# Two transformer layers on one core: query blocks outermost, heads in row and column tiles, three-bank exponentials, and the FFN and next QKV of a finished block run beside the next block's attention

## The chip, the cores and the metric

The kernel runs on one core of a Trainium2 chip. The time is the device time in microseconds (us) of one execution. Engines are named as in the profile: PE is the matmul engine (TensorE), PEld its weight loads, DVE is VectorE, ACT is ScalarE, POOL is GpSimd, SP is SyncE. Each timed run lies beside runs of the kernel before on the same chip.

## The reference, cut to what matters

Two equal layers, each of attention (16 heads of 28) and an FFN with a squared ReLU, over 2048 tokens of width 448; both layers use the same weights.

```python
def attention(x, wqkv, wo):                   # x: 2048 x 448
    q, k, v = split((x @ wqkv), 3, heads=16)  # 16 x 2048 x 28 each
    p = softmax(q @ k.T * 28 ** -0.5)         # 16 x 2048 x 2048
    return merge_heads(p @ v) @ wo
def ffn(x, w1, b1, w2, b2):                   # inner width 1792
    return relu(x @ w1 + b1) ** 2 @ w2 + b2
x = x + attention(layernorm(x), ...);  x = x + ffn(layernorm(x), ...)   # twice
```

The exponentials alone are 2 x 16 x 2048 x 2048 elements: over 128 partitions, 1,048,576 columns for ACT.

## The kernel before: the parts that matter

Each layer is four stages, one after the other: layernorm and QKV, attention, output projection, FFN. Attention goes head by head. A head's 28 query rows are copied into a zeroed buffer of 128 rows, so that a score matmul can use all 128 rows of a K buffer that holds four heads.

```python
order = [(h, kb, u) for h in range(H) for kb in range(NKB) for u in range(NU)]
def issue_scores(h, kb, u):                            # 1024 queries: two banks
    for j in range(2):                                 # L280
        nc.tensor.matmul(sc[:, j*512:(j+1)*512], lhsT=QK_sb[:, mk, kb*P:(kb+1)*P],
                         rhs=qz[:, qc*512:(qc+1)*512], start=True, stop=True)
for i, (h, kb, u) in enumerate(order):
    sc = pending
    pending = issue_scores(*order[i + 1])
    nc.scalar.activation(out=pt, in_=sc, func=AF.Exp, scale=scale)     # L312
    for j in range(2):                                 # L315, column tile by query block
        nc.tensor.matmul(oT[32*qc:32*qc+32, 0:512], lhsT=V_sb[:, kb, h, 0:DHP],
                         rhs=pt[:, j*512:(j+1)*512], tile_position=(0, 32*qc), ...)
# ... cut: head normalisation, a few late QKV tiles ...
attention_layer(); ffn_layer(); attention_layer(); ffn_layer()
```

The softmax here doesn't subtract the row's maximum and nothing guards it: scores larger than these inputs give would overflow.

## Time and profile before

The median is 1514.76 us in 3 runs (1514.45 to 1515.83).

| | before |
|---|---|
| span of the profiled run | 1513.1 us |
| PE, ACT, DVE busy | 89%, 75%, 28% |
| mean granted PE clock | 0.981 |
| in the two attention stages | 1153 us: PE 90%, ACT 87% |
| in all other stages | 360 us, without one exponential |

The busy shares of the page are averages over stages with different limits. The windows by stage, quoted in the prediction, take them apart.

### The profile page before, as it was taken

What the parts mean: (1) busy time and instruction counts of PE and PEld (TensorE: products, weight loads), DVE (VectorE), ACT (ScalarE), POOL (GpSimd) and SP (SyncE); (2) the same over time, 40 slices, a digit from 0 to 9 for tenths busy, and PEclk for the clock granted to TensorE, in tenths of its full rate; (3) what the DMA queues carried; (4) which work ended last, traced back from release to release, by engine and by line L of the source; (5) the groups of instructions that cost most, each with busy time, mean ns of one, the idle gap of its engine ahead of it and who ended that gap; (6) DMA issues with size and microseconds to landing.
All of it is one profiled execution on the core that took longest, in us unless ns stands there. A gap on an engine that the chain in (4) does not pass through costs nothing.

```text
span 1513.1 us, 15919 instructions
## 1 busy us (share of the span) xinstructions
PE 1351.2 (89%) x6214; PEld 438.0 (29%) x6320; DVE 428.9 (28%) x783; ACT 1137.6 (75%) x1273; POOL 29.3 (2%) x41
## 2 busy tenths in 40 slices
PE   6999988888888888699999998888888888887998
PEld 2222222222222222233332222222222222223333
DVE  7333211122111111564452332221111111116432
ACT  4678899988999988354347888899999999882432
POOL 6000000000000000000000000000000000000000
PEclk8999999999999999889999999999999999997999
DMA  6000000000000000110000000000000000002000
GB/s 124 1 0 1 1 1 0 1 0 1 0 1 1 0 1 0 44 43 0 1 1 0 1 1 1 0 1 1 0 1 0 1 0 1 0 1 86 13 16 22
DMA packets 20212, 13.92 MB, mean 9 GB/s; under 512 B 10089, under 2 KB 19242, under 8 KB 20138
## 3 DMA queue, kind: packets, MB, share of 16 engines
q1 hardware_dynamic: 18922, 9.76, 2.6%
q0 software_dynamic: 1216, 3.16, 0.8%
q8 instruction: 49, 0.80, 0.2%
q14 instruction: 25, 0.20, 0.0%
HBM read 11.07 MB, written 1.84 MB: 9 GB/s over the span
## 4 chain that ended last, share of the span: by engine, by line
PE 67%; ACT 24%; issue 5%; DVE 3%; ACTq 0%; DMA 0%; POOL 0%; SPq 0%; POOLq 0%
PE sc L280 25%; ACT pt L312 24%; PE oT L315 16%; PE ph L393 7%; PE py L411 5%; PE pq L208 4%; PE den_b L337 2%; PE pq L224 2%; PE tp L181 2%; PE py L355 2%; DVE st L140 1%; PE oT L332 1%; PE oT L301 1%; PE py L418 1%; DVE recip L341 0%
## 5 line engine op out<-in xcount | busy, mean ns | idle before, releaser
L312 ACT ACTIVATE pt<-sc 128x1024 bf16<-128x1024 f32 x1024 | 1000.1, 1022 | 142.3 <-PE sc L280 126.4
L280 PE MATMUL sc<-qz,QK_sb 128*128 128x512 bf16 x1963 | 603.5, 385 | 0.3 <-issue 0.2
L315 PE MATMUL oT<-pt,V_sb 128*32 128x512 bf16 x2048 | 403.9, 385 | 110.8 <-ACT pt L312 108.7
L315 PEld LDWEIGHTS <-V_sb 128*32 128x32 bf16 x2048 | 152.9, 92 | 518.5 <-issue 518.5
L266 DVE MEMSET qz<- 128x1024 uint32 x32 | 29.2, 912 | 559.5 <-PE sc L280 558.6
L280 PEld LDWEIGHTS <-QK_sb 128*128 128x128 bf16 x2048 | 117.7, 97 | 235.6 <-issue 235.0
L401 ACT ACTIVATE rtmp<-ph,b1col 128x512 bf16<-128x512 f32 x112 | 76.7, 686 | 93.6 <-PE ph L393 93.6
L393 PE MATMUL ph<-xnT,w 128*128 128x512 bf16 (+1 forms) x432 | 124.4, 394 | 1.8 <-issue 0.7
L341 DVE RECIPROCAL recip<-den_b 128x512 f32<-128x512 f32 x32 | 107.4, 3357 | 27.7 <-PE den_b L337 27.5
L411 PE MATMUL py<-w,hact 128*128 128x448 bf16 x448 | 91.0, 353 | 0.0
L208 PE MATMUL pq<-xnT,wqk 128*128 128x512 bf16 (+1 forms) x251 | 83.3, 394 | 3.0 <-ACT xnT L189 1.4
L216 DVE CAST QK_sb<-pq 128x512 bf16<-128x512 f32 x60 | 41.3, 688 | 126.4 <-PE pq L208 126.3
L335 DVE COPY oT_sb<-oT 128x512 f32<-128x512 f32 x32 | 22.1, 692 | 164.5 <-PE oT L332 164.5
L404 DVE TENSOR_TENSOR hact<-rtmp 128x512 bf16<-128x512 bf16 x112 | 47.2, 424 | 65.2 <-ACT rtmp L401 65.2
L181 PE MATMUL tp<-ident,xn 128*128 128x128 bf16 (+1 forms) x256 | 36.8, 261 | 30.3 <-ACT xn L163 28.5
L393 PEld LDWEIGHTS <-w 128*128 128x128 bf16 x448 | 34.7, 97 | 86.6 <-issue 72.7
L411 PEld LDWEIGHTS <-hact 128*128 128x128 bf16 x448 | 40.9, 98 | 41.5 <-issue 7.1
L144 ACT ACT_TABLE_LOAD x3 | 3.8, 1283 | 57.6 <-DVE mv L142 57.6
L208 PEld LDWEIGHTS <-wqk 128*128 128x128 bf16 (+1 forms) x256 | 24.3, 98 | 50.7 <-issue 31.1
L140 DVE BATCH_NORM_STATS2 st<-x_sb 128x6 f32<-128x448 bf16 x64 | 38.3, 607 | 1.3 <-DMA x_sb<-in_A_x_dram 0.8
L163 ACT ACTIVATE xn<-x_sb,nbias,rstd 128x448 bf16<-128x448 bf16 x32 | 24.3, 760 | 19.0 <-PE tp L181 12.7
L224 PE MATMUL pq<-wv,xnT 128*128 128x448 bf16 (+1 forms) x128 | 35.5, 370 | 1.6 <-DVE V_sb L231 1.4
(48 smaller groups left out, 400.9 us busy)
## 6 DMA issues: line engine op xcount, KB each, us to landing
w<-in_B_w_dram SPq DMA_DIRECT2D x2, 1568.0 KB, 12.2
x_sb<-in_A_x_dram SPq DMA_DIRECT2D x4, 448.0 KB
w<-in_B_w_dram POOLq DMA_DIRECT2D x4, 448.0 KB, 7.1
wo_pad<-in_A_wo_dram SPq DMA_DIRECT2D x4, 392.0 KB
w<-in_B_w_dram SPq DMA_DIRECT2D x2, 448.0 KB, 4.5
out_dram<-x_sb SPq DMA_DIRECT2D x8, 112.0 KB, 1.7
out_dram<-x_sb POOLq DMA_DIRECT2D x8, 112.0 KB, 1.9
w<-in_B_w_dram SPq DMA_DIRECT2D x2, 224.0 KB, 6.7
```

The lines of the kernel that those rows point to most:

```text
L140: nc.vector.bn_stats(out=st[:, :], in_=x_sb[:, tb, :])
L181: nc.tensor.transpose(out=tps[dc][:r, j * P:(j + 1) * P], in_=xn[:, dc * P:dc * P + r], identity=ident[:, :],)
L208: nc.tensor.matmul(pq[:, :], lhsT=wqk[0:r, dc, m, :], rhs=xnT[0:r, dc, tcix * 512:(tcix + 1) * 512], start=(dc == 0), stop=(dc == NDC - 1),)
L224: nc.tensor.matmul(pv[:, 0:D], lhsT=xnT[0:r, dc, tb * P:(tb + 1) * P], rhs=wv[0:r, dc, :], start=(dc == 0), stop=(dc == NDC - 1),)
L280: nc.tensor.matmul(sc[:, j * 512:(j + 1) * 512], lhsT=QK_sb[:, mk, kb * P:(kb + 1) * P], rhs=qz[:, qc * 512:(qc + 1) * 512], start=True, s ...
L312: nc.scalar.activation(out=pt[:, :], in_=sc[:, :], func=AF.Exp, scale=scale)
L315: nc.tensor.matmul(oT[32 * qc:32 * qc + 32, 0:512], lhsT=V_sb[:, kb, h, 0:DHP], rhs=pt[:, j * 512:(j + 1) * 512], start=False, stop=False, ...
L341: nc.vector.reciprocal(out=recip[:qrows, :], in_=den_b[:qrows, :])
L393: nc.tensor.matmul(ph[:, :], lhsT=w1[0:r, dc, fc * P:(fc + 1) * P], rhs=xnT[0:r, dc, tcix * 512:(tcix + 1) * 512], start=(dc == 0), stop=( ...
L401: nc.scalar.activation(out=rtmp[:, :], in_=ph[:, :], func=AF.Relu, bias=b1col[:, fc:fc + 1], scale=1.0)
L404: nc.vector.tensor_tensor(out=hact[:, :], in0=rtmp[:, :], in1=rtmp[:, :], op=ALU.mult)
L411: nc.tensor.matmul(py2[:, :], lhsT=hacts[fc][:, j * P:(j + 1) * P], rhs=w2[:, fc, :], start=(fc == 0), stop=False,)
```

## The change

Its intent is to keep ACT at the exponentials from the first to the last. The loop over blocks of 512 queries goes outermost. Four heads lie in four groups of 32 partitions, so that score matmuls of three heads can run in three row tiles and PV matmuls in three column tiles. An exponential covers three PSUM banks (1536 columns). When a query block's attention is done, its projection, FFN and the next layer's QKV are merged into the instruction stream of the next block's attention, by a planner inside the kernel that runs when the program is built and fixes each engine's order. The kernel shares out eight PSUM banks: six for scores, one for the PV sums (`ps_o`), and one (`ps_m`) for all other matmul tiles, which I call filler tiles.

```diff
-order = [(h, kb, u) for h in range(H) for kb in range(NKB) for u in range(NU)]
+    for l in range(2):
+        cut = 4 if l == 0 else NTB - 4
+        for qb in range(NQB):
+            if qb == 0:        # first block: K of the blocks that are ready, then the rest
+                for lo, hi in ((0, cut), (cut, NTB)):
+                    for g in range(G):
+                        passes.append((l, qb, g, range(lo, hi), lo == 0, hi == NTB))
+            else: ...
+    groups = [units[i:i + 3] for i in range(0, len(units), 3)]
...
-            rhs=qz[:, qc * 512:(qc + 1) * 512],
+                r = slice(DHP * hh, DHP * hh + DHP)                       # L416
+                nc.tensor.matmul(sc[:, k * 512:(k + 1) * 512],
+                                 lhsT=K_sb[l][r, g, kb * P:(kb + 1) * P],
+                                 rhs=Q_sb[l][r, g, qb * QB:(qb + 1) * QB],
+                                 start=True, stop=True, tile_position=(DHP * hh, 0))
...
-    nc.scalar.activation(out=pt[:, :], in_=sc[:, :], func=AF.Exp, scale=scale)
+    nc.scalar.activation(out=pt[:, 0:n], in_=gbuf[gi]["sc"][:, 0:n], func=AF.Exp, scale=scale)  # L431, n = 1536
...
+                nc.tensor.matmul(box["t"][DHP * hh:DHP * hh + DHP, :],    # L460
+                                 lhsT=V_sb[l][:, kb, 4 * g + hh, :],
+                                 rhs=gbuf[gi]["pt"][:, k * 512:(k + 1) * 512], ...,
+                                 tile_position=(0, DHP * hh))
...
+    def chain(l, qb):          # spawned when a query block is normalised
+        # projection, layernorm, FFN; in layer 0 also layernorm and QKV of layer 1
+        ...
+    # a filler tile: matmuls into the one bank of ps_m (L335), then its evacuation
...
+        nc.gpsimd.memset(V_sb[0][:], 1.0)                                 # L199
+        nc.gpsimd.memset(V_sb[1][:], 1.0)                                 # L214
```

Smaller parts of it: weights are loaded once and not per layer, b1 is a row of w1, 1/sqrt is done on DVE instead of ACT, and the transposes of a half block share one bank.

## The prediction

> **What bounds the kernel now.** I read the windows by stage first, cut where the exponentials (L312) begin and end: head, attention, output projection, layernorm and FFN, layernorm and QKV, attention, projection, FFN. Columns: stretch, its length, then busy time of PE, PEld, DVE, ACT, POOL.
>
> ```profile
> 0.00:38.00 38.00, 23.24 (x97) 8.98 (x98) 27.81 (x94) 15.81 (x35) 22.74 (x29) 0.87 0.67 123
> 38.00:617.00 579.00, 520.90 (x2227) 158.47 (x2271) 122.71 (x131) 501.41 (x513) 0.00 (x0) 1.00 0.00 1
> 617.00:638.00 21.00, 15.55 (x266) 7.61 (x263) 13.77 (x20) 0.00 (x0) 1.12 (x2) 0.84 0.05 9
> 638.00:766.00 128.00, 120.82 (x535) 45.80 (x543) 66.35 (x196) 56.60 (x100) 0.00 (x0) 0.95 0.08 25
> 766.00:788.00 22.00, 19.48 (x106) 8.26 (x106) 16.55 (x53) 12.54 (x26) 0.00 (x0) 1.00 0.00 0
> 788.00:1362.00 574.00, 516.89 (x2207) 156.63 (x2249) 117.43 (x122) 499.02 (x512) 0.00 (x0) 1.00 0.00 1
> ```
>
> Two attention stages take 1153 us of 1513; PE is busy 90% there and ACT 87%, so neither is free. The other 360 us (38+21+128+22+22+129) run with no exponential at all. Then the costliest groups, which size the units of work, and the chain of waits:
>
> ```profile
> PE 67%; ACT 24%; issue 5%; DVE 3%; ACTq 0%; DMA 0%; POOL 0%; SPq 0%; POOLq 0%
> ...
> L312 ACT ACTIVATE pt<-sc 128x1024 bf16<-128x1024 f32 x1024 | 1000.1, 1022 | 142.3 <-PE sc L280 126.4
> L280 PE MATMUL sc<-qz,QK_sb 128*128 128x512 bf16 x1963 | 603.5, 385 | 0.3 <-issue 0.2
> L315 PE MATMUL oT<-pt,V_sb 128*32 128x512 bf16 x2048 | 403.9, 385 | 110.8 <-ACT pt L312 108.7
> ```
>
> ACT waits 142 us, nearly all for scores; PE waits 111 us for exponentials. They hand work to each other and both lose. The timeline of one steady stretch (start, duration) shows how:
>
> ```profile
> 300.32 0.39 PE L315 MATMUL oT<-pt,V_sb 128*32 128x512 bf16 x2 [0.26 <-ACT pt L312]
> ...
> 300.65 0.61 PE L280 MATMUL sc<-qz,QK_sb 128*128 128x512 bf16 x2
> ...
> 301.24 0.39 PE L315 MATMUL oT<-pt,V_sb 128*32 128x512 bf16 x2
> 301.35 1.94 ACT L312 ACTIVATE pt<-sc 128x1024 bf16<-128x1024 f32 x2 [0.17 <-PE sc L280]
> ```
>
> Two exponentials run without a gap in 1.94 us, so the second starts 0.92 us after the first; then 0.17 us is lost. Start to start on PE, two PV matmuls cost 0.33 us (their two column tiles overlap), two score matmuls 0.59 us (0.54 in the chain), one after the other. PE needs about 0.89 us per unit of 1024 columns and ACT 0.92; with each waiting for the other, 577/512 = 1.13 us results.
>
> Two pieces of the chain of waits carry the cost of tiled and untiled matmuls outside attention: 256 matmuls of the output projection, four row tiles at a time, and 14 of the FFN's second product.
>
> ```profile
> 621.91 14.13 PE py L355 x231
> ...
> 673.00 2.75 PE py L411 x14
> ```
>
> **What the Trainium skill says.** (1) "ScalarE: Activation LUTs", What ACT_TABLE_LOAD costs: 186 ns plus 0.833 ns per element, neighbours overlapping by about 93 ns. The trace agrees closely: 1022 ns at 1024 columns (formula 1039), overlap 100 ns. (2) "TensorE: Matmul & The Clock Gate", Measured speedup vs the span model: four row tiles with a contraction of 32 gave 3.07 times. This trace has such matmuls, the output projection L355 (32 rows, 448 columns): 14.13 us / 64 = 0.22 us per four (the trace lacks a few records, the program has 256), where L411, of the same width, takes 2.75 / 14 = 0.196 each. That is 3.6 times. (3) "TensorEngine Tiling (Array Packing)", Key Properties: a change of tiling mode drains TensorE. The trace fits: L393 needs 1.07 us per four matmuls, one of them on 64 rows; four at 0.22 (L411's rate scaled to 512 columns) would be 0.89, so about 0.1 us per change. (4) The first page, part 3, The mechanism: matmuls start and end in program order. So a merged matmul that waits for its PSUM buffer holds up the scores behind it. The kernel before has little of that to check.
>
> **The change, part by part.** Instruction counts come from the two programs' orders.
>
> Exponentials: 1024 of 1024 columns become 683 of 1536. By the trace's slope, 1.02 + 512 x 0.833 ns = 1.45 us each, 1.35 us start to start. 683 x 1.35 = **922 us**, against 1024 x 0.92 = 942 before if it never waited. The width alone saves only 20 us.
>
> Attention on PE: the scores keep 2048 matmuls, but with 32 rows, three heads side by side: 0.22 + 0.11 for the mode change = 0.33 us instead of 3 x 0.27 = 0.81. PV: three column tiles for about 0.36. So 0.69 us per group, 471 us in all, where 1024 x 0.89 = 911 us stood. The zero-padded queries (32 memsets, 64 copies on DVE) go. ACT becomes the bound with half of PE free.
>
> What fills that half: transposes 256 x 0.08 = 20, QKV 256 x 0.216 + 128 x 0.196 = 80, projection 25, FFN 448 x 0.216 + 480 x 0.196 = 191, denominators 32 x 0.86 = 28: 344 us. About 60 of these lie in the tail and in stalls below; some 285, in about 370 of the 683 groups, lie beside exponentials. PE there: 471 + 285 + 370 x 0.2 (two changes of mode) = 830 of 922 us. It fits on average, but a group with filler has 0.69 + 0.76 + 0.2 = 1.65 us against 1.35. If all that excess counted it would be 370 x 0.3 = 111 us; two score buffers and filler-free neighbours should take half. I add **50 us**.
>
> Stages that stay outside: the order shows where score groups stop for fillers. All fillers share one PSUM bank, so each is serial: 0.87 matmuls + 0.65 evacuation + 0.25 handoff, about 1.8 us.
> - First exponential: first x at 6 us, four statistics 3, rsqrt by twelve small DVE operations 2, normalise, transpose and evacuate twice 6, K and Q of four heads 5: **22 us**.
> - Layer 1 needs K of all blocks at once. Before score group 5, six tiles are serial (11 us against 7 us of exponentials); after group 25 seven tiles (12.6 less 2.7 us queued on ACT); after group 31 eleven (20 less 2.7). Stalls 4 + 10 + 17 = **31 us**.
> - Between layers, after group 351: the rest of an FFN, a layernorm, one K tile, 13 less 2.7; after group 404: two FFN output tiles (2 x 3.75), layernorm 8, K 1.8, less 2.7. **10 + 14 = 24 us**.
> - Tail after the last exponential: PV, copy, denominator 2.3; reciprocal 3.4; multiply 0.7; projection 4 x 1.6; layernorm 8; FFN 14 x 1.75 and 4 x 3.75; output 4.6 (as before, from last addition to end): **65 us**.
>
> Sum: 22 + 922 + 50 + 31 + 24 + 65 = 1114; I state **1110 us**. As a balance: the 360 us without exponentials shrink to 142, attention from 1153 to 972.
>
> **Rivals.** (a) PE becomes the bound. For: 830 of 922 us is 90%, and PE can't reorder past a waiting matmul. Against: row tiles ran at 3.6 times here. If three row tiles ran serially (0.75 us per group), PE would need 1.1 us before fillers, 1120 us in all beside 922: total about 1290. (b) The single PSUM bank for fillers becomes the bound, with DVE behind it: 304 tiles x 1.8-3.8 us and a 3.36 us reciprocal holding it 32 times make 304 x 2.2 + 32 x 4 = 800 us, close enough to ACT to stop PE in places; I'd give it 30 to 60 us more, 1150-1170. (c) Planned order fits better than I think, fillers fully hidden: 1060. (d) DVE as the bound: adding its groups at the durations before (relu 0.69, square 0.42, evacuations 0.69, reciprocals 107 in all) gives about 520 us, half the span; no. (e) Transfers: 9 GB/s mean, and weights are loaded once rather than per layer; they only matter in the head.
>
> **Range and chances.** (c) sets the lower end, (b) the upper: 1055 to 1170. Even serial row tiles leave 15%, so slower needs a fault I don't see.
>
> **What would show it right or wrong.** Right: ACT busy about 990 us (683 x 1.45) and near 10 tenths in the middle of the span; L431 idle for PE about 100-130 us, most of it in the first 110 us and at two gaps midway; score triples in 0.33 us; ACT leading the chain; about 65 us after the last exponential. Wrong: score triples near 0.7 us or PE above 95% busy through the middle (rival a); PE idle behind evacuations spread over the whole span (b); the head's and midway's stalls twice or half my 55 us, as that is counted from an order with durations of another kernel; exponentials not overlapping by 0.1 us (683 x 0.1 = 68 us more).

## The result, and the profile after

The kernel after takes 1145.82 us (median of 4 runs, 1143.03 to 1147.52); the kernel before took 1514.61 us beside it. The ratio is 0.7565, with a 95% interval from 0.7551 to 0.758. Ratios here are the mean time of one kernel's runs over that of the other's of the same rounds, so they are not quite the ratio of the medians. The forecast was 1110 us, within 1055 to 1170: the direction and most of the size are right, and 36 us are missing.

From the page of the kernel after: PE, ACT and the granted clock in 40 slices, then the three groups of attention.

```profile
PE   2876878889898989899789967999889988899646
ACT  1763899999999999999579738899989999899511
PEclk9998876899898998899889978699969986799569
...
L431 ACT ACTIVATE pt<-sc 128x1536 bf16<-128x1536 f32 (+1 forms) x683 | 926.3, 1538 | 112.9 <-PE sc L416 108.9
L416 PE MATMUL sc<-Q_sb,K_sb 32*128 32x512 bf16 x2048 | 298.3, 427 | 92.6 <-ACT pt L431 87.7
L460 PE MATMUL oT<-pt,V_sb 128*32 128x512 bf16 x2048 | 291.1, 429 | 7.1 <-DVE V_sb L373 3.9
```

ACT is full in the middle of the span and has four weak places: the head, a stretch near the tenth of the span, one midway, and the tail. The clock line is new: before, it stood at full speed nearly throughout; now it sinks in many slices, to a mean of 0.876. Its first slice is no measurement: the trace has no clock record before 35.5 us, and four matmuls of a K tile take 1.86 us there (at 23.53 us), against 1.02 us in the tail at full clock. Start to start, an exponential in a run without gaps takes 35.03 us / 26 = 1.347 us (the timeline has such a run at 136 us), just as forecast.

Here are the windows of the kernel after, cut where ACT starts, stops and resumes. Columns: stretch and length, then busy time and count of PE, PEld, DVE, ACT and POOL, the mean granted clock, the DMA's share and rate.

```profile
0.00:29.26 29.26, 6.63 (x30) 2.74 (x30) 25.05 (x61) 4.34 (x5) 18.25 (x16) 1.00 0.73 228
29.26:110.94 81.68, 63.15 (x376) 21.96 (x380) 40.62 (x93) 45.25 (x35) 0.00 (x0) 0.98 0.00 1
110.94:558.86 447.92, 397.14 (x2530) 128.83 (x2551) 196.47 (x320) 433.68 (x320) 0.00 (x0) 0.89 0.00 1
558.86:683.86 125.00, 101.78 (x616) 35.68 (x623) 58.20 (x138) 79.14 (x59) 0.00 (x0) 0.88 0.00 1
683.86:1074.01 390.15, 342.82 (x2109) 107.01 (x2121) 157.38 (x236) 369.96 (x273) 3.38 (x6) 0.85 0.01 4
1074.01:1143.90 69.89, 38.68 (x150) 15.86 (x151) 23.14 (x51) 8.36 (x14) 1.08 (x2) 0.79 0.02 7
```

The third and fifth rows are the steady ones, ACT busy 97% and 95%. (The clock of 1.00 in the first row is the missing record again.) The chain that ended last can't be read for this kernel: on its page 98% of it is "issue", because it follows POOL's queue, which waits for the outputs. I therefore added up ACT's own line, run by run in the timeline. Before the first exponential lie 29.3 us; the exponentials fill 927.0 us; between them are 117.8 us of gaps, of which seven over 2 us make 84.0 and 49 short ones (up to 2 us) make 33.8; after the last lie 69.9 us. The forecast for the same parts: 22, 922, 55 for the long stalls and 50 for the short ones, 65.

### The profile page after: what moved, and what is told of

It reads as the page before. It is cut to its first block, busy times and chain, and to the rows that moved or that the text cites. A ratio compares the mean times of both kernels' runs of the same rounds, so it can differ in the third digit from the quotient of the medians.

```text
span 1143.9 us, 14096 instructions
## 1 busy us (share of the span) xinstructions
PE 950.2 (83%) x5804; PEld 312.1 (27%) x5856; DVE 500.9 (44%) x898; ACT 940.7 (82%) x705; POOL 22.7 (2%) x24
## 4 chain that ended last, share of the span: by engine, by line
issue 98%; POOL 1%; DMA 0%; SPq 0%; POOLq 0%
POOL V_sb L214 1%; DMA x_sb<-in_A_x_dram 0%; SPq L184 0%; POOL out_dram L558 0%; POOL wo L213 0%; POOLq L605 0%; POOL b2w L212 0%; POOL one L211 0%; POOLq L558 0%
## 5 line engine op out<-in xcount | busy, mean ns | idle before, releaser
L431 ACT ACTIVATE pt<-sc 128x1536 bf16<-128x1536 f32 (+1 forms) x683 | 926.3, 1538 | 112.9 <-PE sc L416 108.9
L416 PE MATMUL sc<-Q_sb,K_sb 32*128 32x512 bf16 x2048 | 298.3, 427 | 92.6 <-ACT pt L431 87.7
L460 PE MATMUL oT<-pt,V_sb 128*32 128x512 bf16 x2048 | 291.1, 429 | 7.1 <-DVE V_sb L373 3.9
L416 PEld LDWEIGHTS <-K_sb 32*128 32x128 bf16 x2048 | 86.9, 92 | 347.6 <-issue 340.4
L498 DVE RECIPROCAL rec<-den 128x512 f32<-128x512 f32 x32 | 107.4, 3355 | 64.9 <-PE den L493 64.9
L335 PE MATMUL mt<-xnT,w 128*128 128x512 bf16 x417 | 119.5, 395 | 17.5 <-ACT r L534 9.1
L460 PEld LDWEIGHTS <-V_sb 128*32 128x32 bf16 x2048 | 68.1, 94 | 187.7 <-issue 176.4
L335 PE MATMUL mt<-w,h 128*128 128x448 bf16 x448 | 107.8, 356 | 3.7 <-DVE x_sb L514 2.3
L536 DVE TENSOR_SCALAR r<-mt 128x512 bf16<-128x512 f32 x98 | 67.8, 692 | 89.5 <-PE mt L335 89.5
L542 DVE TENSOR_TENSOR h<-r 128x512 bf16<-128x512 bf16 x112 | 47.5, 424 | 22.9 <-ACT r L534 19.9
```

Source lines behind the costliest of these rows:

```text
L335: nc.tensor.matmul(box["t"][:, 0:n], lhsT=lhsT, rhs=rhs, start=(i + k == 0), stop=(i + k == len(mms) - 1))
L416: nc.tensor.matmul(sc[:, k * 512:(k + 1) * 512], lhsT=K_sb[l][r, g, kb * P:(kb + 1) * P], rhs=Q_sb[l][r, g, qb * QB:(qb + 1) * QB], start= ...
L431: nc.scalar.activation(out=pt[:, 0:n], in_=gbuf[gi]["sc"][:, 0:n], func=AF.Exp, scale=scale)
L460: nc.tensor.matmul(box["t"][DHP * hh:DHP * hh + DHP, :], lhsT=V_sb[l][:, kb, 4 * g + hh, :], rhs=gbuf[gi]["pt"][:, k * 512:(k + 1) * 512], ...
L498: nc.vector.reciprocal(out=rec[:, :], in_=box["t"][:, :])
L536: nc.vector.tensor_scalar(out=r[:, :], in0=t[:, 0:QB], scalar1=0.0, scalar2=None, op0=ALU.max)
```

## The experiments

Ten kernels were run, all made from the kernel after. The theory was that ACT's exponentials set the pace and that the rest of the time is a sum of separate exposed pieces: the head, stalls for K, short waits, the tail. The rivals were that PE's throughput sets the pace, or that the single PSUM bank of the filler tiles does so everywhere. Times are medians of 4 runs in the fast state, or of one run where said, whose state is then unknown. Lines shown are of the profiled run.

### e1: what holds up the head

In the timeline of the kernel after, POOL and DVE in the head:

```profile
3.03 6.92 POOL L199 MEMSET V_sb<- 128x8192 bf16 x1
...
6.58 3.54 DVE L271 TENSOR_SCALAR ve<-mv 128x4 f32<-128x4 f32 x1
...
12.07 6.91 POOL L214 MEMSET V_sb<- 128x8192 bf16 x1
...
12.33 7.09 DVE L300 TENSOR_SCALAR xn<-x_sb,mv,rstd 128x448 bf16<-128x448 bf16 x2
```

The same operation on 4 columns takes 0.14 us for the next block (at 27.06 us), not 3.54. It ends within 0.2 us of the end of one fill of V, the pair below within 0.5 us of the end of the other. The Trainium skill, "SBUF — State Buffer", section Who interferes with whom, says that DVE in a mode that uses both port pairs and GpSimd lock each other out for a whole instruction, and names `tensor_scalar` among the operations that can enter such a mode. These two pairs fit that; the run tests it. The edit leaves POOL only the four padding columns per head, which are all that the result needs:

```diff
-        nc.gpsimd.memset(V_sb[0][:], 1.0)
+        nc.gpsimd.memset(V_sb[0][:, :, :, DH:DHP], 1.0)
-        nc.gpsimd.memset(V_sb[1][:], 1.0)
+        nc.gpsimd.memset(V_sb[1][:, :, :, DH:DHP], 1.0)
```

> GpSimd fills only the four padding columns of each V buffer instead of the whole buffer. Theory: in the head the two 6.9 us memsets hold the port that VectorE needs, so one 0.14 us operation took 3.54 us and a pair of normalisations took 7.09 us instead of 0.7. Freed of that, the first exponential starts at about 19.5 us instead of 29.3, and the whole is about 9.7 us shorter: 1136 us. Rival: VectorE was waiting for the loads of x or the weights in that stretch; then the first exponential stays within 1 us of 29.3 and the time at 1145.

Measured: 1135.98 us, correct; the first exponential starts at 19.53 us. From its timeline:

```profile
3.04 0.95 POOL L199 MEMSET V_sb<- 128x1024 bf16 x1
...
6.58 0.44 DVE L271 TENSOR_SCALAR ve<-mv 128x4 f32<-128x4 f32 x1
...
9.25 0.70 DVE L300 TENSOR_SCALAR xn<-x_sb,mv,rstd 128x448 bf16<-128x448 bf16 x2
```

Both numbers are those expected. The fills cost 9.7 us, and in that time DVE was not waiting for data. Even the short operation shrinks to 0.44 us and not to the 0.14 us that it takes later: a shortened fill runs beside it from 6.06 to 7.00 us.

### e2: the one bank of the filler tiles

The planner may now give a filler tile one of the two score buffers while the score stream is stopped for lack of K, and after its end. The core of the edit:

```diff
+    def pools(self, o):
+        if not isinstance(o.acq, tuple):
+            return [o.acq]
+        return o.acq if self.stopped else o.acq[:1]
...
-            t = Op("PE", 0.6, tr, deps=[x[1] for x in xs], acq=R_m)
+            t = Op("PE", 0.6, tr, deps=[x[1] for x in xs], acq=(R_m, R_sc))
...
-                       deps=list(deps) if i == 0 else [last], acq=R_m if i == 0 else None)
+                       deps=list(deps) if i == 0 else [last], acq=(R_m, R_sc) if i == 0 else None)
```

> While the score stream is stopped for lack of K, and after it has ended, the other matmul tiles may also take the two score buffers. Theory: the single PSUM bank makes each tile serial with its evacuation (1.71 us per FFN tile in the tail), so the tail shrinks from 70 to about 56 us, the stalls of the head from 37 to about 25, the two large stalls midway from 39 to about 25: together some 35 us, 1110 us. Rival: TensorE at half clock or VectorE set the pace in these stretches, not the bank: at most 10 us less.

Measured: 1104.89 us, correct, 41 us less than the kernel after. The profiled run was the slowest of the four (1112.3 us). In it the tail fell from 69.9 to 52.8 us and the three stalls of the head from 37.4 to 21.5. In the tail of the kernel after, twelve of the 14 tiles of the FFN's first product look like this, 1.71 us from one to the next (the first two, at half clock, take longer):

```profile
1106.69 1.02 PE L335 MATMUL mt<-xnT,w 128*128 128x512 bf16 x4 [0.69 <-ACT r L534]
...
1107.76 0.60 ACT L534 ACTIVATE r<-mt 128x512 bf16<-128x512 f32 x1 [1.11 <-PE mt L335]
```

PE waits for the evacuation, then ACT for PE: they never overlap. In e2's tail, PE runs on through eleven tiles and ACT follows every 0.87 us:

```profile
1084.81 10.09 PE L349 MATMUL mt<-xnT,w 128*128 128x512 bf16 x45
...
1086.31 0.60 ACT L554 ACTIVATE r<-mt 128x512 bf16<-128x512 f32 x1 [0.27 <-PE mt L349]
```

But the two large stalls midway, 20.3 and 18.6 us, became 16.9 and 19.2: the bank is a small part of the first and none of the second, and this part of the expectation (25 us for both) failed. The timeline of the kernel after shows two different stalls. In the first (from 558.9 us), the projection tiles of the last block stand on PE between the steps of the layernorm of the block before it, and the additions that empty them stand between its steps on DVE. This is the order that the planner fixed, and the layernorm that K waits for takes 14.9 us, from 560.8 to 575.7. In the second (from 651.7 us) nothing of another block stands between: two FFN output tiles take 7.4 us (ACT still has work for the first 1.8), a layernorm 9.8, the K tile and the first scores 3.4. Neither reading was isolated by a run of its own; e8 shows only that another order of attention, with its other changes, removes the stalls.

### e3 and e9: what row tiles are worth

e3 sends the scores of all heads to row tile 0, one after the other; e9 runs them over all 128 rows, mixing four heads, also one after the other. Their outputs are wrong, which doesn't matter for the times. One run each.

```diff
-                    r = slice(DHP * hh, DHP * hh + DHP)
+                    r = slice(0, DHP)              # e3, with tile_position=(0, 0)
+                    r = slice(0, P)                # e9, without tile_position
```

> All heads' score matmuls use row tile 0 (wrong result on purpose, the same number of matmuls and bytes), so three can't run side by side. Theory: a triple costs about 0.77 us instead of 0.33; TensorE then needs 1.1 us per group before the other work, 1110 us or more in all, and becomes the bound: 1290 to 1350 us, ACT busy below 75%. Rival: the row tiles don't matter because the exponentials hide the scores anyway: below 1170 us.

> Score matmuls over all 128 rows, mixing four heads (wrong result on purpose; as many matmuls, one after the other as in e3). Theory: e3 ran at 0.55 of the clock although TensorE was 95% busy, because a matmul on 32 rows alone counts as little activity; on 128 rows the clock stays above 0.9, a triple costs about 0.75 us and TensorE is the bound: 1240 to 1320 us. Rival: serial score matmuls as such bring the half clock: 0.55 and about 2000 us again.

Measured: e3 1998.23 us, e9 1217.80 us. e3 is far beyond what I expected, and e9, sent to find out why, is below it. From e3's page:

```profile
PE 1899.6 (95%) x5804; PEld 434.7 (22%) x5856; DVE 502.3 (25%) x898; ACT 1001.2 (50%) x705; POOL 22.7 (1%) x24
...
PEclk8965555555555555555555965555555555555559
```

And from e9's:

```profile
PE 1086.1 (89%) x5747; PEld 397.6 (33%) x5856; DVE 501.6 (41%) x898; ACT 966.2 (79%) x705; POOL 22.7 (2%) x24
...
PEclk9999999999999999999979979999999999999969
```

Both run the same number of matmuls of 512 columns in the same order. In e3 PE is busy 95% of the time, and yet it is granted half the clock (mean 0.551); a triple of scores takes 1.39 us there. In e9 the clock is 0.976. So in these two runs the clock doesn't follow PE's busy time as the profile gives it. That it weighs how much of the array works fits both runs, but is an inference: e9 also leaves the row-tile mode, and no run separates the two. Row tiles side by side are worth 72 us against e9 (1217.8 against 1145.8), although e9 had the higher clock (0.976 against 0.876). Most of the other 780 us that e3 lost are probably the clock, at which the other matmuls ran too: a PV triple is 0.61 us there and 0.40 in e9.

### e4: what the low clock costs in the kernel after

In 191 groups that have no filler beside them, the scores are issued twice, with the same result:

```diff
-                for k, (pi, kb, hh) in enumerate(us):
+                for k, (pi, kb, hh) in [*enumerate(us)] * (2 if gi in TWICE else 1):
```

> In 191 groups that have no other matmuls beside them, each score matmul is issued twice (same result), which only adds TensorE work. Theory: the clock is halved because TensorE has too little to do in these stretches, and at half clock the scores, denominators and other tiles come late; with more work the granted clock rises from 0.876 to above 0.92 and the short waits of ACT (42 us in all) shrink by 5 to 20 us: 1125 to 1140 us. Rival: the clock does not follow the amount of work, or the half clock costs nothing: the clock stays and the time is 1145 to 1155.

Measured: 1123.60 us, correct, 22 us less, with 573 more matmuls. The mean clock rose from 0.876 to 0.944. From its page:

```profile
PEclk9998979899999999999889979999989998899779
```

ACT's short waits fell from 33.8 to 11.6 us, the same 22 us; the long stalls and the tail stayed. How the low clock hurts can be read in a sparse stretch of the kernel after:

```profile
169.83 2.08 PE L493 MATMUL den<-oT_sb,sel 128*128 128x512 f32 x2
...
171.84 0.49 PE L416 MATMUL sc<-Q_sb,K_sb 32*128 32x512 bf16 x3
...
172.44 2.79 ACT L431 ACTIVATE pt<-sc 128x1536 bf16<-128x1536 f32 x2 [1.25 <-PE sc L416]
172.58 0.39 PE L416 MATMUL sc<-Q_sb,K_sb 32*128 32x512 bf16 x3
...
172.91 0.40 PE L460 MATMUL oT<-pt,V_sb 128*32 128x512 bf16 x3
```

With three row tiles and three column tiles side by side, PE has about 0.66 us of work per 1.35 us: at full speed a score triple and a PV triple take 0.33 us each, start to start (172.58 to 172.91). That little work lets the clock fall. The fp32 denominator then takes 2.0 us in place of 0.86, longer than one exponential, and ACT stands for 1.25 us. More work made the kernel faster, by keeping the clock up.

### e5 and e6: the width of the exponentials, and more filler banks

Both go back to exponentials of 1024 columns. e5 keeps six score banks as three buffers; e6 has two buffers of two banks, and three banks for filler tiles.

```diff
-    groups = [units[i:i + 3] for i in range(0, len(units), 3)]
+    groups = [units[i:i + 2] for i in range(0, len(units), 2)]
-    ps_sc ... bufs=2 ... [P, 3 * 512]            ps_m ... bufs=1
+    ps_sc ... bufs=3 ... [P, 2 * 512]            # e5
+    ps_sc ... bufs=2 ... [P, 2 * 512]            ps_m ... bufs=3      # e6
```

> Exponentials of 1024 columns again, three score buffers of two banks (six banks as before), all else kept. Theory: ACT's own time grows by 1024 x 0.92 - 683 x 1.345 = 23 us only, but every group brings its two changes of mode, so TensorE needs 1024 x 0.66 = 676 us for scores and PV instead of about 471, with the other work about 1035 us, and passes ACT: 1200 to 1260 us. Rival: only ACT's fixed cost per instruction matters: 1146 + 23 = 1169 us.

> Exponentials of 1024 columns with two score buffers (four banks), so the other matmul tiles get three PSUM banks instead of one. Theory: tail, head and midway stalls lose some 50 us against the run with one such bank, but TensorE stays the bound in the middle: 1150 to 1210 us. Rival: the single bank is what holds the whole kernel: below 1120 us, better than the 1536-column version.

Measured: e5 1335.72 us, e6 1253.79 us, both correct. Both are slower than the kernel after, and both lie above the ranges that I expected (1200 to 1260 and 1150 to 1210). ACT's own time grew by 31 us in e5 (927 to 958), near the 23 expected, so the fixed cost per exponential is not the point. The gaps grew by 147 us. One of them alone is 80.8 us (at 619 us), and the program's order tells why: all 14 FFN tiles and the four output tiles of the block before the last stand between two score groups there. The planner lets in a filler only if it delays the next scores by little, and a shorter exponential leaves less room. So e5 does not measure the width by itself; it measures it with this planner. With three filler banks (e6) the tail falls to 61.4 us and the long stalls to 67 us, but the short waits reach 97 us. Both expectations of a bank-bound kernel (below 1120 us) and of an ACT-bound one (1169 us) are out.

### e7: without the merging

Projection, FFN and next QKV of all four blocks run after the layer's attention, block after block. (To make room, one buffer less for `pt` and for `xnT`.)

```diff
-        if len(norm_done[l, qb]) == G:
-            pl.spawn(4, chain(l, qb))
+        if qb == NQB - 1 and len(norm_done[l, qb]) == G:
+            pl.spawn(4, chains(l))       # for qb in range(NQB): yield from chain(l, qb)
```

> Projection, FFN and the next layer's QKV of all four blocks run after the layer's attention instead of beside it (four blocks' oTn kept; one buffer less for pt and for xnT to make room). Theory: a block's chain takes 86 us in layer 1 and 62 us in layer 2 by the tile times of the tail; 345 and 250 us come to stand alone in place of about 46 and 70: 1560 to 1650 us, slower than the kernel before. Rival: what runs beside the exponentials delays them as much as it saves: below 1400 us.

Measured: 1565.89 us, correct, one run: slower than the kernel before. ACT in its 40 slices:

```profile
ACT  2739999999999911121119838999999996101101
```

Between the layers ACT stops for 82.0, 83.0, 85.3 and 25.4 us, and the tail is 245.7 us; a block's chain takes about 83 us (86 expected), and 61 in the tail (62 expected). Against this form, merging is worth 420 us, more than the whole gain of the change: the other parts alone, with one filler bank, lose 51 us against the kernel before. But the form is a slow one. Its stops and tail make 521 us, where the kernel before did the same work outside attention in 322 us (21 + 128 + 22 + 22 + 129, its windows after the head). Against an unmerged form as fast as that, merging would be worth about 220 us by this estimate; no run shows it. With hardly any fillers beside the scores, the granted clock in the two attention stretches is 0.65 and 0.64 (0.89 and 0.85 in the steady rows of the kernel after), which fits the reading of e4.

### e8 and e10: the causes together

e8 combines e1, e2 and the repeated scores of e4 (for its own sparse groups) with another order of attention. In layer 1 the first query block takes K block by block, so that it never needs K of a block whose QKV has not come up. In layer 2 the first two query blocks take the K of finished blocks first, which leaves the last chain time. e10 is e8 without the repetition.

```diff
+        if l == 0:
+            parts = [(0, 0, 4), (0, 4, 8), (0, 8, 12), (0, 12, 16), (1, 0, 16), (2, 0, 16), (3, 0, 16)]
+        else:
+            parts = [(0, 0, 8), (1, 0, 8), (0, 8, 12), (1, 8, 12), (0, 12, 16), (1, 12, 16),
+                     (2, 0, 16), (3, 0, 16)]
+        for qb, lo, hi in parts:          # partial PV sums are kept and added
```

> Small padding fills, idle score banks for other tiles, scores twice in groups with nothing beside them, and another order of attention: in layer 1 the first query block takes K block by block, in layer 2 the first two query blocks take the finished K blocks first. Theory: the causes add: head -10, tail -17, clock -22, stalls of K from 84 to about 15: 1146 - 118 = 1028 us, 1015 to 1050. Rival: the stalls only move, as the chain of the last block needs its time wherever it stands: 1070 to 1090.

> e8 without the second issue of the scores. Theory: the half clock comes back in the sparse stretches and with it the short waits: 1035 to 1050 us against 1022, clock about 0.9. Rival: with the stalls gone the other work fills the sparse stretches and the repetition does nothing: 1022 within 5 us.

Measured: e8 1021.98 us (1017.47 to 1024.09), correct: 0.6732 of the kernel before, and 124 us less than the kernel after. e10 1051.90 us, correct, 2 us above the range expected. In e8, the long stalls are down from 84.0 to 7.5 us, the first exponential starts at 18.4 us, the tail is 56.8 us. So the stalls were not bound to come back elsewhere. The repetition is worth 30 us here (clock 0.902 to 0.966), a little more than in e4: filling the stalls did not fill the sparse stretches. The windows of e8, from the first exponential, and one in the middle:

```profile
18.43:100.00 81.57, 74.33 (x514) 26.94 (x521) 46.51 (x112) 76.20 (x59) 0.00 (x0) 1.00 0.08 23
...
500.00:700.00 200.00, 180.26 (x1298) 57.58 (x1306) 84.13 (x166) 198.52 (x148) 0.00 (x0) 0.96 0.00 1
```

ACT is busy 93% and 99%, where the kernel after had 55% (its second row) and 63% (its fourth).

## Why the prediction was right, and where its sizes were off

The forecast lies in its range, and its main mechanisms hold. That it is within 36 us is in part luck: the short waits were put 16 us too high, which covered a third of the 46 us by which the other terms were too low. Four readings in it need a note. The exponentials of the kernel before begin at 43.4 us, after a table load, not at the edge of the window at 38; they take 571 us per layer, and 371 us are without them, not 360. The 0.833 ns per column, called the trace's slope there, is the figure of the page cited; a single exponential of the kernel after takes 1.45 us, as worked out. The 3.6 times of point (2) mixes clocks: the window of the output projection, 617 to 638, was granted 0.84, that of L411, 638 to 766, 0.95. And "the first page" in point (4) is the page of point (2), on TensorE.

- **ACT's exponentials as the pace: right.** 922 us forecast, 927.0 measured; 1.35 us start to start, 1.347 measured. The bill "683 x 1.45 = 990 us busy" that I set as a check was wrong in itself: the page counts overlapping instructions once and shows 926.3.
- **Merging as the larger gain: right.** I had the time without exponentials fall from 360 to 142 us. Measured: 29.3 + 84.0 + 69.9 = 183 us. e7 shows that the merging carries it, though not how much a faster unmerged form would have left for it.
- **Row tiles and column tiles: right at full clock.** A triple takes 0.33 us. My term for both, 471 us, assumed the clock of the kernel before. The page's 298.3 + 291.1 = 589 us busy can't be set against it: it counts each triple to its modelled end, 0.39 and 0.40 us where the next starts after 0.33. At full clock, 683 of each would be 540 us busy, so about 50 are the low clock. That PE, relieved of work, would be granted a lower clock is what I left out. e4 wins back 22 us of what it cost, all of it in ACT's short waits, and its clock, 0.944, is still below the 0.981 of before.
- **Short waits: 50 us forecast, 33.8 measured.** The size was too large by half, and the cause was another: I counted groups with filler, and two thirds of what was measured are the low clock (33.8 to 11.6 us in e4). ACT's idle time for scores, 108.9 us on the page, is within the 100 to 130 that I named.
- **Head: 22 forecast, 29.3 measured.** I took the DVE operations at their durations before and missed that POOL's fills of V would hold two of them up. Without that it is 19.5 us (e1).
- **Stalls for K in the head: 31 forecast, 37.4 measured** (6.8, 11.3 and 19.4 for my 4, 10 and 17): the count of tiles from the program's order was a sound method.
- **Midway: 24 forecast, 46.5 measured** (20.3, 18.6, 5.4 and 2.2). This is the worst term. For the first stall, forecast 10, I added the steps of one block's layernorm as if nothing stood between them; the timeline shows the next block's projection between them (14.9 us for my 8), and a clock at half in part of that stretch. For the second, forecast 14, the steps are those that I listed, but the layernorm takes 9.8 us for my 8, and the K tile with the first scores 3.4 for my 1.8. The last two stalls I did not foresee. e2 shows that the filler bank, which I had made responsible, has little part there.
- **Tail: 65 forecast, 69.9 measured.** Most FFN tiles took 1.71 and 3.71 us for my 1.75 and 3.75. The denominator and the projection ran at half clock: 2.36 us from one projection tile to the next for my 1.6, 3 us in four. The layernorm took 9.8 us for my 8 here too.

The differences add up: 7 + 5 + 29 - 16 + 5 = 30, which leads from 1114 to the profiled 1144 us.

**The rivals.** (a) PE as the bound was rightly put aside for the change as it is. Its number, 1290 us with serial row tiles, was wrong twice: serial scores over 128 rows, near full clock, make 1218 us (e9), and in a single row tile 1998 us (e3). (b) The filler bank holds up the tail and the head (33 us in e2), but has little part in the stalls midway, and in the steady rows ACT is busy 97% and 95% in spite of it; so as the bound of the whole it falls. (c) Full hiding as a lower end of 1060 us lay above what e8 reaches, since e8 takes away stalls that I had treated as given. (d) and (e), DVE and transfers as bounds, find no support: DVE is 44% busy and the DMA moves 7 GB/s.

One check could not be made: "ACT leading the chain". The chain of this kernel runs along POOL's queue.

## What to carry to other kernels

First make the engine that can't be avoided work without a gap: count the stretches where it has nothing to do, and move other work beside it; here that was worth 420 us against the same kernel without it (some 220 by estimate against a faster unmerged form), while the wider instruction changed ACT's own time by only 31 us (e5). Then read the granted clock in every stretch, for a change that relieves the matmul engine can lower its clock, as here from 0.981 to 0.876, and look at the order that the program fixes for each engine where the gaps are. The single bank for all side work cost most where nothing else ran, in the head and the tail (33 us in e2).

## What the Trainium skill lacked or had wrong

- "TensorE: Matmul & The Clock Gate", Part 1, ties the clock to how busy PE is. It doesn't say that score matmuls on 32 rows, one tile at a time, can leave the clock low: e3 had PE busy 95% at a mean clock of 0.551, e9, with 128 rows and without row tiles, 89% at 0.976 (one run each).
- The same page, and "TensorEngine Tiling (Array Packing)", recommend row tiles and don't warn that the relief can lower the clock: 0.981 before, 0.876 after, and 22 us shorter when the same scores were issued twice in the sparse stretches (e4).
- "TensorEngine Tiling (Array Packing)" says that a change of mode drains PE, without a size. Here, at full clock, a triple of scores or of PV takes 0.33 us from one start to the next, mode change included.
- "SBUF — State Buffer" was right on the shared port. It gives no example for fills at a kernel's start: one memset of 6.9 us lengthened an operation on four columns to 3.54 us, and two such fills cost 9.7 us.
- No page has the cost of mixing tiles of two chains in the fixed order of PE and DVE. By the timeline it drew out the layernorm in the first stall midway to 14.9 us, where one alone takes 9.8; no run isolates it.
